# A radix-4 fold of the even half of a d-transform, with the front of the kernel re-ordered around it

## The chip, the cores and the metric

The kernel runs on one core of one Trainium2 chip. The metric is device microseconds for one execution of the program, the median of three runs. Five engines of the core matter here, and the profile's names are used for them: PE (TensorE, matrix products; PEld is its weight loads), DVE (VectorE), ACT (ScalarE), POOL (GpSimd) and SP (SyncE, which issues most DMAs). PE writes its products into PSUM, and DVE or ACT copy them out from there.

## The reference

The kernel computes a gated mix of two branches on the same x (2048 tokens of 1024 features):

```python
g = sigmoid((x * gate_w).sum(-1))
a = irfft2(rfft2(x) * (w_r + 1j * w_i))            # spectral branch
Bu = einsum("bld,pd->blp", x, B_bar)               # state-space branch
h_t = Lam_bar * h_(t-1) + Bu_t                     # for all 2048 tokens
b = 2 * einsum("blp,dp->bld", h, C).real + x * Dskip
out = g * a + (1 - g) * b
```

All inputs and the output are bf16, except that some small parameters come as float32.

## The kernel before

The work of PE, DVE and ACT is emitted inside a guard that keeps each of these three engines to the written order: an instruction that waits holds up everything written after it on its engine. So the order of the Python text is the schedule, and this case is about that order.

**The front, steps 0 to 15.** x is read as 16 blocks of 128 tokens. For each block `turn_x` (L663, letter T) transposes it with eight small PE products into PSUM, and ACT copies it into `xQ`. `fold` (L670, letter f) forms the sum and the difference of the two halves of the feature axis with two DVE instructions of 512 elements a partition (`preT`). `fd` (L342, letter F) is the transform along d: eight products of 512 columns into one PSUM tile `ps_fd`, four for the even class of frequencies (from the sums) and four for the odd class (from the differences), and one copy into `X1` by ACT, or by DVE for blocks 3, 5 and 7. `s1` (L352, letter S) is the first stage of the transform along the tokens: four products into `ps_s1`, one copy into `A1` (by DVE for blocks below 8, by ACT from 8 on), and a DMA of `A1` to DRAM. `front()` (L782) does one step: it walks through the letters of `plan` (L780), where F at step j is the transform of block j+1 and S is the token stage of block j; where the plan has no entry the letters are fFS. Then it issues the loads that `order` (L772) lists for the step, and then it advances `tables` by `pieces`.

`ps_fd`, `ps_s1` and the gate's `zps_g` take turns in one pool of two PSUM buffers, `psA`. A product that opens a buffer waits for the copy that empties the one before it there.

**The tables.** `sincos` (L825) makes sines and cosines in three parts: DVE reduces the angle, ACT does the absolute value and the sine, ACT does the cosine. It is used once for a few small vectors (`s2c`, `c2c`, L844), which feed a chain of about 25 small DVE instructions (L847 to L869), and then in `make_tab` (L210) for four pairs of table rows. Each `make_tab` has five parts: the angle on DVE (L215, L828, L830); absolute value and sine on ACT; cosine and two scalings `t1` on ACT (L226); two scalings `t2` on ACT and two DVE instructions that need `t1` (L232); two DVE instructions that need `t2` (L237).

**The units.** `unit(c, q)` (L301) computes Bu for a chunk c of 256 tokens and one half q of the states: two halves (real, imaginary) of 32 products of 256 columns into `psu`, and an ACT copy into `h`. `halves(ssm, n)` emits the next n halves of a list (L770) in which eight units stand first, and then the `early` tiles, which multiply finished states with C. When a unit is complete, `recur` (L254) puts its recurrence on a list of DVE pieces: two products with the tables, two joins, two scans, the carry, two products, two outputs. Each piece has a cost written down; `vector(us)` (L321) adds us to a budget and emits pieces while the budget is positive. `vector(4.2)` stands in steps 9 to 15, `vector(3.0)` after each of the halves that follow.

**After the front.** `gfnet` goes on with short stages whose names are the letters of L892: four halves of units beside "w"; "a" transposes the saved columns `Acol` into `aps`, from which DVE copies `Bcol` (L423); the first half of `early(0)`; then "z", whose products `zps` (L430) read `Bcol`. In the DVE's order `Bcol` stands behind everything that was written before it: all folds, copies and tables of the front and all pieces that the budget has let out by then.

`keep_A1(j)` (L367) saves columns of four `A1` tiles on DVE before ACT overwrites the first of them at block 12. `gate()` (L708) is emitted at step 10. SP issues its DMAs in the order written: x, the constants G and T2, the transposing loads of B (`load_B`) and of C (`load_C`), and the stores of `A1`.

Of the kernel before, what the change touches and what calls it, by code (L numbers as in the profile page):

```python
# [21 lines left out]
K = 512  # L22
# [15 lines left out]
def _host_consts():  # L38

    d = np.arange(K)[:, None] + 0.5  # L40
    G = np.zeros((2, K, 2, H))
    for cls in range(2):
        k = 2 * np.arange(H)[None, :] + cls
        ang = 2 * np.pi * d * k / D
        G[cls, :, 0] = np.cos(ang)
        G[cls, :, 1] = -np.sin(ang)
    G[0, :, 1, 0] = (-1.0) ** np.arange(K)

    n = np.arange(H)[None, :] + 0.5
    Gi = np.zeros((2, 2, 2, P, H))  # L50
    for cls in range(2):
        for kb in range(2):
            k = 2 * (P * kb + np.arange(P)[:, None]) + cls
            ang = 2 * np.pi * k * n / D
            Gi[cls, kb, 0] = 2.0 * np.cos(ang)
            Gi[cls, kb, 1] = -2.0 * np.sin(ang)
    Gi[0, 0, 0, 0] = 1.0
    Gi[0, 0, 1, 0] = (-1.0) ** np.arange(H)
    Gi /= float(D * S)
    pf = np.arange(P)  # L60
    s1 = (32 * (pf % 64) + 16 * (pf // 64))[:, None, None]
# [36 lines left out]
    return dict(  # L98
        G=b16(G.reshape(2, 4, P, K).transpose(2, 0, 1, 3)),
        Gi=b16(Gi.reshape(8, P, H).transpose(1, 0, 2)),  # L100
        T2=b16(np.concatenate([Ts, Tc, -Ts], axis=2)),
        K3=b16(np.stack([Kc, Ks], axis=1)),
        MT=b16(np.concatenate([-Mim, Mre, Mim], axis=2)),
        KRS=b16(np.concatenate([K2, R2, Sel.reshape(P, 4 * P)], axis=1)),
        JP=b16(np.stack([J, P0], axis=1)),
    )
# [3 lines left out]
def kernel(  # L110
# [78 lines left out]
    xn = [CT[i // 4][:, 2 * (i % 4):2 * (i % 4) + 2, :] for i in range(8)]  # L189
    x_v = x.rearrange("(p j) d -> p j d", j=16)  # L190
    fft = {}
    fft["G"] = pre.tile([P, 2, 4, K], BF16, name="G_sb")
    raw = t3p.tile([P, 6 * D], BF16, name="raw")
    fft["T2"] = raw[:, 0:3 * D].rearrange("p (j m) -> p j m", m=192)

# [141 lines left out]
    def gfnet():  # L337
# [3 lines left out]

        def fd(j):  # L342
            ps = psA.tile([P, 2, K], FP32, name="ps_fd", tag="ps")
            for cls in range(2):
                for d4 in range(4):
                    nc.tensor.matmul(ps[:, cls, :], lhsT=preTs[j][:, 4 * cls + d4, :], rhs=G_sb[:, cls, d4, :],  # L346
                                     start=(d4 == 0), stop=(d4 == 3))
            X1 = gta.tile([P, 2, K], BF16, name="X1")
            (nc.vector.tensor_copy if j in (3,5,7,) else nc.scalar.copy)(out=X1.rearrange("p r (i c) -> p r i c", c=2), in_=ps.rearrange("p c (r i) -> p r i c", r=2))  # L349
            X1s[j] = X1  # L350

        def s1(j):  # L352
# [10 lines left out]
            (nc.vector.tensor_copy if j < 8 else nc.scalar.copy)(out=A1, in_=psa)  # L363
            A1s[j] = A1
            nc.sync.dma_start(out=t1_w[j], in_=A1)

# [291 lines left out]
        yield 3.9  # L658


    preTs = {}

    def turn_x(j):  # L663
        pt = psX.tile([P, 8, P], BF16, name="pt")
# [3 lines left out]
                       in_=pt.rearrange("p d (c q g) -> p d c g q", c=NCH, g=2))  # L668

    def fold(j):  # L670
        preTs[j] = gta.tile([P, 8, P], BF16, name="preT", bufs=3)
        lo, hi = (x_gjq[:, :, d:d + 4, :, j, :].rearrange("p c d g q -> p d g c q") for d in (0, 4))
        to = preTs[j].rearrange("p d (g c q) -> p d g c q", g=2, c=NCH)
        nc.vector.tensor_add(out=to[:, 0:4], in0=lo, in1=hi)  # L674
        nc.vector.tensor_sub(out=to[:, 4:8], in0=lo, in1=hi)  # L675

    A1_4 = gta.tile([P, 4, 2, K], BF16, name="A1", bufs=1)
    idle = A1_4[:, 3, 0]
# [6 lines left out]

    keep_warm(8)
    load_x(0)
    for cls in range(2):
        nc.sync.dma_start(out=fft["G"][:, cls], in_=cG[:, cls])
    load_T2(0, 2)  # L690
    load_x(1)
    load_x(2)
    load_T2(2, 8)
    for i in range(3, 8):
        load_x(i)
    load_T2(8, 16)
    assert step() == "front"
    for j in range(2):
        turn_x(j)
# [66 lines left out]
    def halves(gen, n):  # L766
# [3 lines left out]
    ssm = chain(unit(0, 0), unit(0, 1), unit(1, 0), unit(1, 1), unit(2, 0), unit(2, 1), early(0), early(1), unit(3, 0), early(2), unit(3, 1), early(3), unit(4, 0), early(4), unit(4, 1), early(5), unit(5, 0), early(6), unit(5, 1), early(7), unit(6, 0), unit(6, 1), early(8), early(9))  # L770

    order = {  # L772
        **{j: [(load_B, n)] for j, n in ((2, 1), (3, 1), (4, 1), (5, 2), (6, 2), (7, 2), (8, 2), (9, 2))},
        10: [(load_B, 3), (load_small,)],
        **{j: [(load_C, j - 11)] for j in range(11, 15)},
    }
    at = [0]
    tables = iter(())

    plan = {0: "FSTfTf", 1: "TSFfT", 2: "TFfTS", 3: "TFfTS", 4: "TFfTS", 5: "TFfTS", 6: "TFfTS", 7: "TFfTS"}  # L780

    def front(pieces=0):  # L782
        j = at[0]
# [50 lines left out]
        yield  # L834
        nc.scalar.activation(out=cos_out, in_=kk, func=ACT.Sin, scale=-2.0 * PI_LO, bias=chpi[:shape[0]])

    front()

    ang2 = sp.tile([P, 2, 8], FP32, name="ang2")
    nc.vector.tensor_copy(out=ang2[:, 0], in_=thp)  # L840
    nc.vector.tensor_scalar_mul(out=ang2[:, 1], in0=thp, scalar1=float(TC))
    s2c = sp.tile([P, 2, 8], FP32, name="s2c")
    c2c = sp.tile([P, 2, 8], FP32, name="c2c")
    for _ in sincos(sp, ang2, [P, 2, 8], s2c, c2c, "a2"):  # L844
        front()
# [25 lines left out]
    tables = chain(*(make_tab(jp) for jp in range(4)))  # L871
    while at[0] < 16:
        j = at[0]
        front(0 if j < 4 else 1 if j < 6 else 2 if j < 10 else 3)
        if j >= 8:
            halves(ssm, 1)
        if j >= 9:
            vector(4.2)
        if j == 10:
            gate()  # L880
        if j == 15:
            for _ in tables:
                pass
            tctx.close()
        if j == 7:
            xctx.close()
            pools["u"] = ctx.enter_context(tc.tile_pool(name="psU", bufs=2, space=PSUM, reuse_waits="tile"))
        if j == 3:
            load_Wcols()
# [94 lines left out]
```

## Time and profile before

| | us |
|---|---|
| median of 3 runs | 340.34 (340.12 to 340.48) |
| the profiled execution | 340.26 |
| its span in the trace | 338.5 |
| PE busy | 327.9 (97%) |
| DVE busy | 283.5 (84%) |
| ACT busy | 167.3 (49%) |

The profiled execution is 1.8 us longer than its span; these lie before the first and after the last instruction. A busy PE is not a PE at its peak: the records of its products overlap. So the table says which engines are candidates, and the stretches and the single instructions have to say which one sets the end, and where. Most rows of the trace give a start, a duration, the engine and line, the operation, what it writes and reads, and in square brackets how long the engine sat idle before it and what ended that.

### The profile page before, as it was taken

The numbers are of one execution on the slowest core, as the hardware profiler recorded it, in microseconds if no ns is written. First come the engines' busy times: TensorE is split into PE (matmuls) and PEld (weight loads), VectorE is DVE, ScalarE is ACT, GpSimd is POOL, SyncE is SP. The second block draws the span as 40 slices with busy tenths as digits, with TensorE's granted clock in tenths as the row PEclk, the third lists the DMA queues.
The fourth block names the chain that finished last, engine by engine and source line by source line (L and its number), as shares of the span: only waits on it lengthen the run. The fifth ranks groups of instructions, "written<-read, shape, count | busy, mean of one in ns | idle before, by whom it ended". The sixth has DMA issues, their size and how long they took to land.

```text
span 338.5 us, 6167 instructions
## 1 busy us (share of the span) xinstructions
PE 327.9 (97%) x2446; PEld 212.0 (63%) x2446; DVE 283.5 (84%) x385; ACT 167.3 (49%) x211; POOL 32.7 (10%) x64
## 2 busy tenths in 40 slices
PE   8989899979999999999999999999999999999995
PEld 3445465656985574847566575869945876565552
DVE  2679948999999999999997999199699939999741
ACT  3697598836241245656557452546632243433510
POOL 1382011140000000000000000000000011121410
PEclk9999999999999999999999999999999999999999
DMA  7999999999890346899999955898114004556892
GB/s 268 404 200 144 244 220 213 129 202 263 261 230 11 95 123 145 254 243 282 259 270 242 218 174 151 225 188 217 62 33 122 35 4 71 102 86 124 131 194 102
DMA packets 83581, 58.71 MB, mean 173 GB/s; under 512 B 54328, under 2 KB 74304, under 8 KB 83424
## 3 DMA queue, kind: packets, MB, share of 16 engines
q1 hardware_dynamic: 80304, 55.64, 66.5%
q0 software_dynamic: 3168, 2.66, 8.3%
q8 instruction: 19, 0.31, 0.4%
q14 instruction: 10, 0.08, 0.1%
q10 hardware_dynamic: 80, 0.01, 0.0%
HBM read 30.49 MB, written 17.83 MB: 143 GB/s over the span
## 4 chain that ended last, share of the span: by engine, by line
PE 81%; DVE 13%; ACT 3%; issue 2%; ACTq 0%; DVEq 0%
PE ps_y L580 29%; PE psu L308 28%; PE ps_h L580 4%; PE ps_id L611 4%; PE ps_fd L346 3%; PE ps_is L519 2%; PE ps_is L494 2%; PE ps_s L470 2%; PE ps_is L495 2%; DVE CT L363 2%; PE ps_y L584 2%; DVE h L278 1%; DVE preT L674 1%; PE psw L684 1%; DVE preT L675 1%
## 5 line engine op out<-in xcount | busy, mean ns | idle before, releaser
L308 PE MATMUL psu<-xQ,BT 128*128 128x256 bf16 x1024 | 116.2, 273 | 0.8 <-ACT ye L598 0.5
L308 PEld LDWEIGHTS <-BT 128*128 128x128 bf16 x1024 | 99.0, 98 | 17.4 <-issue 4.5
L580 PE MATMUL ps_y<-CT,h 128*128 128x512 bf16 x448 | 101.3, 379 | 0.0
L580 PEld LDWEIGHTS <-h 128*128 128x128 bf16 x512 | 49.4, 98 | 55.3
L278 DVE TENSOR_TENSOR_SCAN h<-rz,h 128x1024 bf16<-128x1024 f32 x32 | 71.9, 2278 | 0.2
L310 ACT CAST h<-psu 128x1024 bf16<-128x1024 f32 x32 | 32.3, 1010 | 51.0 <-PE psu L308 51.0
L263 DVE TENSOR_TENSOR xQ<-h,tab 128x4096 bf16<-128x4096 bf16 x12 | 27.4, 2287 | 14.2 <-ACT h L310 14.2
L266 DVE TENSOR_TENSOR h<-h,tab 128x4096 bf16<-128x4096 bf16 (+1 forms) x20 | 37.3, 1864 | 0.8
L626 POOL DMA_DIRECT2D BT<-y_scratch x10 | 11.9, 1194 | 238.8 <-DVE BT L620 227.1
L598 ACT ACTIVATE ye<-ps_y,omg 128x512 f32<-128x512 f32 x20 | 12.7, 684 | 43.4 <-PE ps_y L584 35.7
L346 PE MATMUL ps_fd<-G_sb,preT 128*128 128x512 bf16 x128 | 30.4, 379 | 1.6 <-ACT X L349 1.0
L346 PEld LDWEIGHTS <-preT 128*128 128x128 bf16 x128 | 12.0, 97 | 15.5 <-issue 2.8
L472 ACT CAST X<-ps_s 128x1024 bf16<-128x1024 f32 x16 | 16.2, 1014 | 8.7 <-PE ps_s L470 8.7
L667 ACT COPY xQ<-pt 128x1024 bf16<-128x1024 bf16 x16 | 15.6, 1016 | 2.6 <-PE pt L666 2.5
L521 ACT CAST ZT<-ps_is 128x1024 bf16<-128x1024 f32 x16 | 15.5, 1024 | 2.2 <-PE ps_is L519 2.2
L497 ACT CAST C<-ps_is 128x1024 bf16<-128x1024 f32 x16 | 16.1, 1007 | 0.0
L611 PE MATMUL ps_id<-raw,ZT 128*128 128x256 bf16 x128 | 15.9, 273 | 0.0
L349 ACT CAST X<-ps_fd 128x1024 bf16<-128x1024 f32 x13 | 13.2, 1013 | 5.5 <-PE ps_fd L346 5.4
L580 PE MATMUL ps_h<-CT,h 128*128 128x512 bf16 x64 | 14.5, 379 | 0.0
L611 PEld LDWEIGHTS <-ZT 128*128 128x128 bf16 x128 | 12.4, 98 | 2.2
L674 DVE TENSOR_TENSOR preT<-xQ 128x512 bf16<-128x512 bf16 x16 | 7.4, 460 | 5.8 <-ACT xQ L667 5.8
L494 PE MATMUL ps_is<-X,raw 128*128 128x512 bf16 x32 | 12.1, 379 | 0.0
(189 smaller groups left out, 350.0 us busy)
## 6 DMA issues: line engine op xcount, KB each, us to landing
y_scratch<-ye SPq DMA_DIRECT2D x20, 256.0 KB, 2.7
CT<-in_A_x_dram SPq DMA_DIRECT2D x8, 512.0 KB, 5.6
Bb<-turn_scratch SPq DMA_DIRECT2D x16, 256.0 KB, 3.8
turn_scratch<-C SPq DMA_DIRECT2D x16, 256.0 KB, 4.5
raw<-turn_scratch SPq DMA_DIRECT2D x16, 256.0 KB, 4.7
Wb<-in_A_w_r_dram SPq DMA_DIRECT2D x32, 127.8 KB, 4.0
Wb<-in_A_w_i_dram SPq DMA_DIRECT2D x32, 127.8 KB, 3.8
out_dram<-BT SPq DMA_DIRECT2D x14, 256.0 KB, 2.6
```

The costliest lines, as they stand in the source:

```text
L263: nc.vector.tensor_mul(out=tmps["s"], in0=u[:, ::-1], in1=bc(i))
L266: nc.vector.tensor_mul(out=u, in0=u, in1=bc(i))
L278: nc.vector.tensor_tensor_scan(out=seg, data0=rz[:, js.start + j:js.start + j + 4].rearrange("p j t -> p (j t)"), data1=seg, initial=0.0, ...
L308: nc.tensor.matmul(psu[:, j, :], lhsT=BT[4 * q + j][:, ri, d8, :], rhs=xQ[:, c, d8, :], start=(d8 == 0), stop=(d8 == 7))
L310: nc.scalar.copy(out=hs[c][:, ri, 4 * q:4 * q + 4].rearrange("p b (q j) -> p b q j", j=32), in_=psu.rearrange("p b (j q) -> p b q j", j=32))
L346: nc.tensor.matmul(ps[:, cls, :], lhsT=preTs[j][:, 4 * cls + d4, :], rhs=G_sb[:, cls, d4, :], start=(d4 == 0), stop=(d4 == 3))
L472: nc.scalar.copy(out=X2, in_=ps2)
L494: nc.tensor.matmul(psc[:, h, :], lhsT=MT_sb[:, b, 64:192], rhs=UV[0][:, h, :], start=True, stop=False)
L497: nc.scalar.copy(out=C1.rearrange("p h (c i) -> p h c i", c=2), in_=psc.rearrange("p h (i c) -> p h c i", c=2))
L580: nc.tensor.matmul(psy, lhsT=hs[c][:, ri, jb, P * tq:P * (tq + 1)], rhs=CT[ri][:, jb, 512 * dh:512 * (dh + 1)], start=(i == 0), stop=False)
L611: nc.tensor.matmul(pse[:, slot, :], lhsT=ZT_t[:, i, tb, :], rhs=fft["Gi"][:, i, :], start=(kb == 0), stop=(kb == 1))
L667: nc.scalar.copy(out=x_gjq[:, :, :, :, j, :].rearrange("p c d g q -> p d c g q"), in_=pt.rearrange("p d (c q g) -> p d c g q", c=NCH, g=2))
```

## The change

The even half of the transform along d is folded once more. The even class needs the sums of the two halves of the feature axis; its frequencies are themselves split into two classes, which need the sums and the differences of the two halves of those sums. `G` shrinks from 8 blocks of 512 columns to 4 of 512 (odd) and 4 of 256 (even), the odd ones loaded first. `fd` does the odd class first, then four products of 256 columns. `fold` gains two DVE instructions, which run over the pair of blocks at once from block 2 on, and block by block for 0 and 1. With it go other moves: which engine copies what (`X1` of block 7 and `A1` of blocks 6 and 7 go from DVE to ACT), the plan (all turns of x within steps 0 to 4), the loads (eight B loads in steps 1 to 3, T2's second half in step 3), the small sines and cosines (steps 5 and 6 in place of 1 and 2), the tables (steps 7 to 12 in place of 4 to 12), the halves of units (steps 6 to 13 in place of 8 to 15) and the recurrence pieces (from step 8 in place of 9).

```diff
         def fd(j):
             ps = psA.tile([P, 2, K], FP32, name="ps_fd", tag="ps")
-            for cls in range(2):
-                for d4 in range(4):
-                    nc.tensor.matmul(ps[:, cls, :], lhsT=preTs[j][:, 4 * cls + d4, :], rhs=G_sb[:, cls, d4, :],
-                                     start=(d4 == 0), stop=(d4 == 3))
+            Go = G_sb[:, 0:4 * K].rearrange("p (d n) -> p d n", d=4)
+            Ge = G_sb[:, 4 * K:4 * K + 4 * H].rearrange("p (e d n) -> p e d n", e=2, d=2)
+            for d4 in range(4):
+                nc.tensor.matmul(ps[:, 1, :], lhsT=preTs[j][:, 4 + d4, :], rhs=Go[:, d4, :], start=(d4 == 0), stop=(d4 == 3))
+            for e in range(2):
+                for d2 in range(2):
+                    nc.tensor.matmul(ps[:, 0, H * e:H * (e + 1)], lhsT=preTs[j][:, 2 * e + d2, :], rhs=Ge[:, e, d2, :],
+                                     start=(d2 == 0), stop=(d2 == 1))
             X1 = gta.tile([P, 2, K], BF16, name="X1")
-            (nc.vector.tensor_copy if j in (3,5,7,) else nc.scalar.copy)(out=X1.rearrange("p r (i c) -> p r i c", c=2), in_=ps.rearrange("p c (r i) -> p r i c", r=2))
+            (nc.vector.tensor_copy if j in (3, 5) else nc.scalar.copy)(
+                out=X1.rearrange("p r (m e c) -> p r m e c", e=2, c=2),
+                in_=ps.rearrange("p c (e r m) -> p r m e c", e=2, r=2))
...
-            (nc.vector.tensor_copy if j < 8 else nc.scalar.copy)(out=A1, in_=psa)
+            (nc.vector.tensor_copy if j < 6 else nc.scalar.copy)(out=A1, in_=psa)
...
     def fold(j):
-        preTs[j] = gta.tile([P, 8, P], BF16, name="preT", bufs=3)
+        if j % 2 == 0:
+            pairs["t"] = gta.tile([P, 2, 8, P], BF16, name="preT", bufs=2)
+            pairs["s"] = gta.tile([P, 2, 4, P], BF16, name="sums", bufs=1)
+        preTs[j] = pairs["t"][:, j % 2]
...
-        nc.vector.tensor_add(out=to[:, 0:4], in0=lo, in1=hi)
-        nc.vector.tensor_sub(out=to[:, 4:8], in0=lo, in1=hi)
+        nc.vector.tensor_sub(out=apart(preTs[j])[:, 4:8], in0=lo, in1=hi)
+        nc.vector.tensor_add(out=apart(pairs["s"][:, j % 2]), in0=lo, in1=hi)
+        rs = slice(j % 2, j % 2 + 1) if j < 2 else slice(0, 2)
+        if j < 2 or j % 2:
+            s_lo, s_hi = pairs["s"][:, rs, 0:2], pairs["s"][:, rs, 2:4]
+            nc.vector.tensor_add(out=pairs["t"][:, rs, 0:2], in0=s_lo, in1=s_hi)
+            nc.vector.tensor_sub(out=pairs["t"][:, rs, 2:4], in0=s_lo, in1=s_hi)
...
-    load_T2(8, 16)
...
     order = {
-        **{j: [(load_B, n)] for j, n in ((2, 1), (3, 1), (4, 1), (5, 2), (6, 2), (7, 2), (8, 2), (9, 2))},
-        10: [(load_B, 3), (load_small,)],
+        1: [(load_B, 4)],
+        2: [(load_B, 2)],
+        3: [(load_B, 2), (load_T2, 8, 16), (load_Wcols,)],
+        **{j: [(load_B, 2)] for j in range(4, 8)},
+        10: [(load_small,)],
...
-    plan = {0: "FSTfTf", 1: "TSFfT", 2: "TFfTS", 3: "TFfTS", 4: "TFfTS", 5: "TFfTS", 6: "TFfTS", 7: "TFfTS"}
+    plan = {0: "FSTfTf", 1: "TSFfTT", 2: "TFfTST", 3: "TFfTfST", 4: "TFTfST"}
...
-    front()
+    for _ in range(5):
+        front()
...
-    for _ in sincos(sp, ang2, [P, 2, 8], s2c, c2c, "a2"):
-        front()
+    turns = sincos(sp, ang2, [P, 2, 8], s2c, c2c, "a2")
+    next(turns)
+    front()
+    xctx.close()
+    pools["u"] = ctx.enter_context(tc.tile_pool(name="psU", bufs=2, space=PSUM, reuse_waits="tile"))
+    next(turns)
+    front()
+    halves(ssm, 1)
+    next(turns, None)
...
     while at[0] < 16:
         j = at[0]
-        front(0 if j < 4 else 1 if j < 6 else 2 if j < 10 else 3)
+        front({7: 4, 8: 4, 9: 3, 10: 3}.get(j, 2))
+        if j < 14:
+            halves(ssm, 1)
         if j >= 8:
-            halves(ssm, 1)
-        if j >= 9:
             vector(4.2)
         if j == 10:
             gate()
-        if j == 15:
-            for _ in tables:
-                pass
-            tctx.close()
...
+    for _ in tables:
+        pass
+    tctx.close()
```

More of the change, by code (lines that the diff above doesn't have):

```diff
@@ L47, in _host_consts @@
     G[0, :, 1, 0] = (-1.0) ** np.arange(K)
+    Ge = np.stack([G[0, :H, :, e::2] for e in range(2)])
+    Go = np.stack([G[1, :, :, e::2] for e in range(2)], axis=1)
     n = np.arange(H)[None, :] + 0.5
@@ L98, in _host_consts @@
     return dict(
-        G=b16(G.reshape(2, 4, P, K).transpose(2, 0, 1, 3)),
+        G=b16(np.concatenate([Go.reshape(4, P, 4 * K // 4).transpose(1, 0, 2).reshape(P, 4 * K),
+                              Ge.reshape(2, 2, P, H).transpose(2, 0, 1, 3).reshape(P, 4 * H)], axis=1)),
         Gi=b16(Gi.reshape(8, P, H).transpose(1, 0, 2)),
@@ L191 @@
     fft = {}
-    fft["G"] = pre.tile([P, 2, 4, K], BF16, name="G_sb")
+    fft["G"] = pre.tile([P, 4 * K + 4 * H], BF16, name="G_sb")
     raw = t3p.tile([P, 6 * D], BF16, name="raw")
@@ L658, in own_tile @@
         yield 3.9
-    preTs = {}
+    preTs, pairs = {}, {}
     def turn_x(j):
@@ L670, in fold @@
     def fold(j):
-        preTs[j] = gta.tile([P, 8, P], BF16, name="preT", bufs=3)
+        if j % 2 == 0:
+            pairs["t"] = gta.tile([P, 2, 8, P], BF16, name="preT", bufs=2)
+            pairs["s"] = gta.tile([P, 2, 4, P], BF16, name="sums", bufs=1)
+        preTs[j] = pairs["t"][:, j % 2]
         lo, hi = (x_gjq[:, :, d:d + 4, :, j, :].rearrange("p c d g q -> p d g c q") for d in (0, 4))
-        to = preTs[j].rearrange("p d (g c q) -> p d g c q", g=2, c=NCH)
-        nc.vector.tensor_add(out=to[:, 0:4], in0=lo, in1=hi)
-        nc.vector.tensor_sub(out=to[:, 4:8], in0=lo, in1=hi)
+        apart = lambda t: t.rearrange("p d (g c q) -> p d g c q", g=2, c=NCH)
+        nc.vector.tensor_sub(out=apart(preTs[j])[:, 4:8], in0=lo, in1=hi)
[5 more added lines that the diff above has]
+            nc.vector.tensor_sub(out=pairs["t"][:, rs, 2:4], in0=s_lo, in1=s_hi)
     A1_4 = gta.tile([P, 4, 2, K], BF16, name="A1", bufs=1)
@@ L687 @@
     load_x(0)
-    for cls in range(2):
-        nc.sync.dma_start(out=fft["G"][:, cls], in_=cG[:, cls])
+    for part in (slice(0, 4 * K), slice(4 * K, 4 * K + 4 * H)):
+        nc.sync.dma_start(out=fft["G"][:, part], in_=cG[:, part])
     load_T2(0, 2)
@@ L880 @@
             gate()
-        if j == 15:
-            for _ in tables:
-                pass
-            tctx.close()
[L885 to L889, printed above, removed]
+    for _ in tables:
+        pass
+    tctx.close()
     for q in range(4, 8):
```

## The prediction

> **What bounds the kernel now.** I read the busy times by stretch first (columns: PE, PEld, DVE, ACT and POOL busy with instruction counts, granted PE clock, DMA share, GB/s).
>
> ```profile
> 12.35:18.90 6.55, 5.90 (x53) 3.36 (x51) 4.56 (x13) 5.24 (x7) 2.19 (x12) 1.00 1.23 387
> 18.90:41.40 22.50, 20.07 (x157) 10.42 (x155) 22.11 (x56) 16.64 (x24) 8.74 (x15) 1.00 1.12 182
> 41.40:51.67 10.27, 10.27 (x78) 6.90 (x78) 4.76 (x14) 9.98 (x16) 1.83 (x3) 1.00 1.05 205
> 51.67:71.50 19.83, 19.44 (x164) 12.49 (x161) 19.52 (x29) 13.28 (x20) 5.00 (x7) 1.00 1.11 187
> 71.50:104.50 33.00, 31.69 (x275) 24.67 (x275) 31.48 (x47) 15.09 (x16) 0.33 (x4) 1.00 0.93 221
> 104.50:130.00 25.50, 25.50 (x197) 15.76 (x196) 24.38 (x41) 7.32 (x11) 0.00 (x0) 1.00 0.29 85
> 130.00:334.00 204.00, 203.24 (x1462) 133.10 (x1461) 172.41 (x179) 94.05 (x114) 11.95 (x10) 1.00 0.68 161
> ```
>
> From 104.5 on PE has no hole worth naming, so whatever PE starts late there ends late by as much. From 18.9 to 104.5 the DVE is full too, except in 41.4 to 51.67. Next the instructions in order of time, where the two engines meet:
>
> ```profile
> 45.39 0.91 DVE L232 SCALAR_TENSOR_TENSOR tab<-cs_f,cr,t 128x256 bf16<-128x256 f32 x2 [3.26 <-ACT t L226]
> ...
> 71.75 1.01 ACT L363 CAST A<-ps_s 128x1024 bf16<-128x1024 f32 x1 [4.43 <-DVE Acol L371]
> ...
> 72.81 0.61 PE L358 MATMUL ps_s<-X,raw 64*128 64x512 bf16 x4 [1.70 <-ACT A L363]
> ...
> 103.90 0.69 DVE L269 TENSOR_TENSOR h<-h,su 128x1024 bf16<-128x1024 bf16 x1
> 104.51 0.21 DVE L423 COPY Bcol<-aps 32x128 bf16<-32x128 bf16 x1
> 104.75 0.17 DVE L424 TENSOR_SCALAR Bcol<-Bcol 32x64 bf16<-32x64 bf16 x1
> ...
> 105.27 0.56 PE L430 MATMUL zps<-Bcol,K_sb 32*128 32x16 bf16 x16
> ```
>
> At 71.75 ACT waits for the DVE, and PE loses 1.7 us behind it. At 105.27 PE starts zps, which reads Bcol; the DVE finished it at 104.92. The margin is 0.35 us. So the kernel is bound by the DVE's written order up to Bcol and by PE after it. My prediction is when the DVE reaches Bcol in the new order.
>
> **Prices** (start-to-start, from the order of time): a fold half 0.34; an S copy on DVE 1.14, an X copy 1.22; angle, rounding, subtraction of a table 1.7; L232 and L237 0.8 a pair; on ACT a copy 0.95 to 1.0, absolute value 0.54, sine 0.54, cosine 0.69, t1 0.9, t2 0.9. On PE a T takes 0.55, an S 0.55, a half unit 3.55 with its gap. ps_y needs 3.45 for 16 products of 512 columns, psu 3.49 for 32 of 256: 215.6 and 109.1 ns each. An F goes from 1.83 to about 1.35.
>
> **What PE gains.** 16 x 4 products x 106.5 ns = 6.8 us, if PE is what one waits for.
>
> **What the DVE gets.** No pair instruction is in the trace. The nearest row is a fold half with as many elements, 0.34; the ends are 0.31 (half of L269's 0.61 for 1,024 elements) and 0.69 (L830, as many float32 elements). I take 0.34. From 0.34 and 0.61 a half-size one is some 0.07 + 0.135 = 0.21. So 14 x 0.34 + 4 x 0.21 = 5.6 (ends 5.2 and 11.1); at the dear end all waits below stay and Bcol is 5.5 later. Removed: one X and two S copies, 3.5. These go to ACT, which is busy half the time. The five-dimensional X copy is taken at ACT's 1.01 a copy; doubled, it would put about 3 us on the chain below, and I see no gain. Recurrence: the budget is 8 x 4.2 in place of 7 x 4.2 ahead of the same 4 x 3.0. Worked through piece by piece, before reaches Bcol after the first join of chunk 1's second half (L269 above); after lets the second join, the carry and both scans out too: 0.7 + 0.2 + 4.5 = 5.4. So 5.6 - 3.5 + 5.4 = 7.5 us more DVE work stands ahead of Bcol.
>
> **The steps to the first unit.** Queue by queue, each instruction starts at the latest of its engine, its input and its buffer. Steps 0 to 4 now hold 14 turns in place of 10. F(1) starts at 8.7 and F(2) at 13.4, its even products held by the pair sums until 14.85. Then ACT copies X2 and two turns until 17.75, the first of which (16.8) frees the buffer for turn 7, behind which F(3) stands: 17.4 to 18.75. The DVE, done with fold 4 at 16.4, idles until then. From 18.8 it runs: X3 1.2, fold 5 1.36, S2 1.14, folds 6 and 7 2.05, S3 1.15, to 25.7; a wait of 0.7 for F(5), which stands behind five ACT copies from 19.4 on (24.4); from 26.4 X5 1.2, fold 8 0.7, S4 1.14, angle 0.55, fold 9 1.36, S5 1.14, to 32.5. S(6) needs the buffer that S5's copy empties: 32.55. The first unit starts at 33.15; before, at 40.32. That is the visible gain.
>
> **The new wait.** The small cosine is written behind the first half unit's ACT copy. ACT keeps its order: unit until 36.7, copy until 37.8, cosine until 38.1 (before, c2c ended at 21.87). The DVE has only fold 10 (0.7) meanwhile and idles 4.9 us; behind it waits all of the chain of small vectors, tables and recurrence.
>
> **From 38.1 to Bcol, on the DVE.** Small chain 3.2 (21.79 to 25.05 before); folds 11 to 15 5.45; four tables at 3.25 = 13.0; recurrence quarters 12.4 + 12.4 + 12.5, and 8.45 of the fourth = 45.75 (84.86 to 99.92 shows one); Acol 0.35, the Wc chain 1.3, dgD 1.15, gate 0.9. Sum 71.1. Waits: at steps 7 and 8 four table parts are emitted in a row, so L232 waits for ACT's absolute value, sine, cosine and the first t1 with nothing between: 2.35 each (3.26 before, once). At step 10 L237 waits for t2, which stands behind the h, X and A copies: 2.3. At step 11 0.8. Sum 7.8. Bcol: 38.1 + 71.1 + 7.8 = 117.0, against 104.5.
>
> **Can PE hide it?** No, since ACT hands the DVE's lateness on. The DVE comes to table 2's angle at 38.1 + 3.2 + 1.36 (fold 11) + 1.7 + 2.35 + 0.8 (table 0) + 0.7 + 0.1 + 0.8 + 1.7 + 2.35 + 0.8 (step 8) + 5.95 (five recurrence pieces) + 1.36 + 0.8 + 1.7 (step 9) = 63.8. ACT's absolute value waits for that; behind it stand 2.7 of table work, the copy of unit (0,1) and X11. The gate's products need X11's buffer, so PE, done with unit (1,0)'s first half near 62, starts them at 68.4. S(11) needs the gate's buffer, whose copy stands behind table 3's sine: the DVE ends that angle at 63.8 + 2.24 + 0.7 + 0.8 + 2.3 + 0.8 + 1.7 = 72.3, and ACT's 0.54 + 0.54 + 0.95 + 1.1 make it 75.5. From there PE is dense: three halves, three F, three S, then F15, X15, S15; Wrev at 94.3 (86.86 before), two units to 108.8, the first half of early(0) to 112.3. The old stall of 1.70 at S13 is gone, since PE is now the later one there. Then zps waits for Bcol, and comes 12.5 us late. The work after it is the same, and the DVE, 5.4 ahead in its pieces, makes no new stall. **Sum: 340.26 + 12.5 = 352.8 us.** The profiled execution is 0.08 below the median of the runs, which I leave out.
>
> The granted clock is 1.00 in every stretch, and PE's longest wait in the rows is 1.70 us. The Trainium skill, "TensorE: Matmul & The Clock Gate", Part 1: The HAM clock gate, says that an idle window of about 3.4 us halves PE's clock until it has been busy for as long again. By that rule the holes of 6 and 7 us above cost, as an estimate, some 2 us of PE each (half the clock for 3.4 us), inside time that PE waits anyway; by the rows, nothing.
>
> **The other moves.** SP: the four B transposes at step 1 stand behind the store of block 1's A1 (its copy ends at 15.7) and take about 1.4 each, so the stores of blocks 2 and 3 slip by up to a microsecond, which nothing reads before the front is over. The eight B parts for the first unit are issued by 30 and land about 5 later, needed at 33.15 and 38.8; the other eight by 44, needed at 44 and 52. T2's second half is issued near 30 and needed at 44. Less G and the later T2 take 0.64 MB out of the opening: no turn waits for x in my steps, so it gives nothing. POOL's column loads stay at step 3. If B came late instead, the first unit and the cosine would slip by as much.
>
> **Rivals.** (1) The table waits are covered, because ACT runs ahead of my queues: 7.8 less, Bcol 109.2, 345.0 us. For it: ACT is half idle. Against: its order is written, and 45.39 shows the wait already. (2) The DVE does not decide and the 6.8 us arrive: 333.5 us. For it: 41.4 to 51.67 holds 5.5 us of DVE idle that a better order could fill. Against: 7.5 us of work and 4.9 of wait come in; it decides only if the DVE reaches Bcol before 104.5. (3) A gain eaten exactly, the same time: 340.3, Bcol at 104.5 by chance. (4) Pair sums or the X copy at their dear ends, or a slower PE after its holes: 5 to 6 us more, 358.
>
> **How the numbers follow.** The forecast 0.55 (349 to 357: first unit and waits off by 4 in all), rival 1 0.22 (343 to 349), rival 4 0.11, rival 2 0.09, rival 3 0.03. Range 343 to 359, which holds the forecast, rival 1 and half of rival 4. A measurement of this kernel tells about 0.2% from no change; by cases: faster 0.09, same 0.03, slower 0.88.
>
> **What would show it.** Right: first psu near 33; c2c's cosine behind the first h copy, the DVE idle about 5 us ahead of cTC; idle ahead of L232 at two tables; a PE hole of 6 us or more ahead of zps_g; Bcol near 117 with zps right behind; no new holes after. Wrong: zps before 104, or PE waiting there for something other than Bcol; a first unit after 37 would mean that I mis-read the opening.

## The result, and the profile after

After takes **356.2 us** (354.99 to 356.32) beside 340.26 us for before on the same chip (340.12 to 340.48): a ratio of 1.046, 95% interval 1.0436 to 1.0483. The profiled execution of after is 356.13 us with a span of 354.4, 15.9 more than the span of before. The forecast was 352.8 with a range of 343 to 359, and 0.88 on slower.

The first lines of after's page (busy time and share of the span; then the granted clock in 40 slices; then the shares of the chain that ended last):

```profile
PE 327.7 (92%) x2446; PEld 214.1 (60%) x2446; DVE 285.4 (81%) x400; ACT 170.7 (48%) x214; POOL 33.4 (9%) x64
...
PEclk9999999689999699999999999999999999999999
...
PE 69%; DVE 21%; ACT 7%; issue 2%; DVEq 0%; ACTq 0%
```

PE is busy for as long as before (327.9 us there), although its products hold 6.8 us less work at full clock. The clock row explains it: two slices stand at 6, where before has a 9 in every slice. Hence a busy time must be read together with the clock under which it was spent. The chain's share of DVE is 21%; before, the page has 13%.

The busy times of after by stretch (columns as in the prediction):

```profile
18.90:41.40 22.50, 20.64 (x185) 13.78 (x184) 16.25 (x51) 16.95 (x20) 7.89 (x13) 1.00 1.11 213
...
62.00:76.00 14.00, 6.53 (x44) 2.47 (x43) 12.43 (x21) 9.63 (x15) 2.97 (x4) 0.63 1.09 206
...
95.00:117.12 22.12, 17.57 (x146) 13.93 (x145) 21.50 (x36) 5.55 (x6) 0.00 (x0) 0.96 0.67 171
117.12:123.00 5.88, 5.88 (x31) 2.50 (x31) 5.78 (x10) 0.00 (x0) 0.00 (x0) 0.58 0.00 0
130.00:334.00 204.00, 201.57 (x1478) 134.44 (x1477) 174.59 (x179) 97.01 (x119) 9.55 (x8) 1.00 0.63 153
```

The DVE, full in 18.9 to 41.4 before (22.11 of 22.5), has 6.25 us of idle time there now. PE has lost its dense order: 6.53 of 14 us in 62 to 76, and 4.55 us of idle time up to 117.12. Behind 117.12 the granted clock is 0.58 with a PE that is busy all the time. From 130 to 334 PE misses 2.4 us; before, 0.76.

Single instructions of after, in order of time:

```profile
38.77 0.17 DVE L875 TENSOR_TENSOR cTC<-c2c,r_sb 128x8 f32<-128x8 f32 x1 [4.81 <-ACT c2c L854]
...
46.81 0.91 DVE L235 SCALAR_TENSOR_TENSOR tab<-cs_f,cr,t 128x256 bf16<-128x256 f32 x2 [2.23 <-ACT t L229]
...
64.11 0.63 ACT L851 ACTIVATE rot_kk<-ang 128x512 f32<-128x512 f32 x1 [7.01 <-DVE ang L849]
...
68.52 3.60 PE L728 MATMUL zps_g<-xQ,gw 128*32 128x512 bf16 x32 [6.69 <-ACT X L356]
...
116.88 0.19 DVE L432 COPY Bcol<-aps 32x128 bf16<-32x128 bf16 x1
...
117.12 0.57 PE L439 MATMUL zps<-Bcol,K_sb 32*128 32x16 bf16 x16 [4.56 <-DVE Bcol L432]
117.63 5.79 PE L589 MATMUL ps_y<-CT,h 128*128 128x512 bf16 x16
...
197.69 2.29 DVE L266 TENSOR_TENSOR xQ<-h,tab 128x4096 bf16<-128x4096 bf16 x1 [5.49 <-ACT h L313]
...
203.69 0.39 PE L503 MATMUL ps_is<-X,raw 128*128 128x512 bf16 x1 [1.68 <-DVE X L488]
```

The whole 15.9 us can be added up from these rows and those of before. zps starts at 117.12 in place of 105.27: **11.85 us**. The 16 products of ps_y behind it take 5.79 us in place of 3.63 under the lower clock: **2.2 us**. Near 203.7 PE waits 1.68 us (and 2.17 for its weights) for the DVE's X (L488), which had no such wait before: **1.84 us** by the offset between the two kernels, which goes there from 14.03 to 15.87 and stays so to the end.

### The profile page after: what moved, and what is told of

Same layout as the page of the kernel before. It is cut to its first block, busy times and chain, and to the rows that moved or that the text cites. A ratio compares the mean times of both kernels' runs of the same rounds, so it can differ in the third digit from the quotient of the medians.

```text
span 354.4 us, 6189 instructions
## 1 busy us (share of the span) xinstructions
PE 327.7 (92%) x2446; PEld 214.1 (60%) x2446; DVE 285.4 (81%) x400; ACT 170.7 (48%) x214; POOL 33.4 (9%) x64
## 4 chain that ended last, share of the span: by engine, by line
PE 69%; DVE 21%; ACT 7%; issue 2%; DVEq 0%; ACTq 0%
PE ps_y L589 26%; PE psu L311 21%; DVE h L281 4%; PE ps_h L589 4%; PE ps_id L620 3%; DVE h L269 2%; PE ps_is L528 2%; DVE su L266 2%; PE ps_is L503 2%; PE ps_is L504 2%; PE ps_s L479 2%; PE ps_y L593 2%; ACT h L313 1%; ACT xQ L676 1%; PE psw L701 1%
## 5 line engine op out<-in xcount | busy, mean ns | idle before, releaser
L589 PE MATMUL ps_y<-CT,h 128*128 128x512 bf16 x448 | 103.4, 385 | 0.0
L266 DVE TENSOR_TENSOR xQ<-h,tab 128x4096 bf16<-128x4096 bf16 x12 | 27.4, 2287 | 20.4 <-ACT h L313 20.4
L350 PE MATMUL ps_fd<-G_sb,preT 128*128 128x512 bf16 x64 | 17.3, 395 | 2.6 <-DVE ang L218 1.5
L356 ACT CAST X<-ps_fd 128x1024 bf16<-128x1024 f32 x14 | 14.2, 1014 | 3.9 <-PE ps_fd L353 3.7
L620 PE MATMUL ps_id<-raw,ZT 128*128 128x256 bf16 x128 | 15.9, 273 | 0.0
L620 PEld LDWEIGHTS <-ZT 128*128 128x128 bf16 x128 | 12.4, 98 | 2.2
L503 PE MATMUL ps_is<-X,raw 128*128 128x512 bf16 x32 | 12.1, 379 | 1.7 <-DVE X L488 1.7
L487 DVE TENSOR_TENSOR V<-X,Wb 128x1024 bf16<-128x1024 bf16 x16 | 10.9, 679 | 2.9 <-issue 2.9
L367 PE MATMUL ps_s<-X,raw 64*128 64x512 bf16 x64 | 9.7, 380 | 2.7 <-DVE CT L372 1.1
```

Of the source, the lines that this page charges most:

```text
L266: nc.vector.tensor_mul(out=tmps["s"], in0=u[:, ::-1], in1=bc(i))
L350: nc.tensor.matmul(ps[:, 1, :], lhsT=preTs[j][:, 4 + d4, :], rhs=Go[:, d4, :], start=(d4 == 0), stop=(d4 == 3))
L503: nc.tensor.matmul(psc[:, h, :], lhsT=MT_sb[:, b, 64:192], rhs=UV[0][:, h, :], start=True, stop=False)
L589: nc.tensor.matmul(psy, lhsT=hs[c][:, ri, jb, P * tq:P * (tq + 1)], rhs=CT[ri][:, jb, 512 * dh:512 * (dh + 1)], start=(i == 0), stop=False)
L620: nc.tensor.matmul(pse[:, slot, :], lhsT=ZT_t[:, i, tb, :], rhs=fft["Gi"][:, i, :], start=(kb == 0), stop=(kb == 1))
```

## The experiments

The first two take the change apart, the next four its loss; one prices the copies, and the rest try to keep the gain. The runs of one version differ by 1 to 4 us, so its median and its one profiled execution can differ by more than a microsecond; where that matters both are given.

**The transform alone.** The order, loads and copies of the kernel before, with the smaller G, the new fd and the pair instructions of fold. `X1` of block 7 and `A1` of blocks 6 and 7 stay on the DVE. The core of the edit to before:

```diff
-            for cls in range(2):
-                for d4 in range(4):
-                    nc.tensor.matmul(ps[:, cls, :], lhsT=preTs[j][:, 4 * cls + d4, :], rhs=G_sb[:, cls, d4, :],
...
+            for d4 in range(4):
+                nc.tensor.matmul(ps[:, 1, :], lhsT=preTs[j][:, 4 + d4, :], rhs=Go[:, d4, :], start=(d4 == 0), stop=(d4 == 3))
...
+        if j < 2 or j % 2:
+            s_lo, s_hi = pairs["s"][:, rs, 0:2], pairs["s"][:, rs, 2:4]
+            nc.vector.tensor_add(out=pairs["t"][:, rs, 0:2], in0=s_lo, in1=s_hi)
+            nc.vector.tensor_sub(out=pairs["t"][:, rs, 2:4], in0=s_lo, in1=s_hi)
```

> The kernel before with the radix-4 transform alone: same plan, same loads, same copies (X1 of blocks 3, 5, 7 and A1 of blocks below 8 on DVE), same tables and budgets; only G, fd and fold are the new ones. Theory (the DVE's written order up to Bcol sets the end): the pair sums put 14 x 0.34 + 4 x 0.21 = 5.6 us on the DVE ahead of Bcol, nothing on it is removed, so Bcol slides from 104.5 to about 110 and zps waits for it: 340.3 + 5 = about 345. Rival (PE sets the end): 64 products of half width save 6.8 us: 333.5. A time within 1 us of 340.3 would say that the DVE's idle time between 41 and 52 us took the pair sums in.

Measured: 344.35 us, ratio 1.0093 [1.0061, 1.0125]. From its trace:

```profile
74.94 1.04 PE L353 MATMUL ps_fd<-G_sb,preT 128*128 128x256 bf16 x4 [2.78 <-DVE preT L691]
...
77.42 5.49 PE L311 MATMUL psu<-xQ,BT 128*128 128x256 bf16 x32
...
105.98 0.17 DVE L741 CAST gB<-g_bf 128x16 f32<-128x16 bf16 x1 [2.11 <-ACT g_bf L740]
...
110.74 0.56 PE L439 MATMUL zps<-Bcol,K_sb 32*128 32x16 bf16 x16
```

The same place in the trace of before:

```profile
100.51 0.17 DVE L724 CAST gB<-g_bf 128x16 f32<-128x16 bf16 x1 [0.59 <-ACT g_bf L723]
```

The DVE reaches Bcol at 109.97, 5.5 us later than in before, as the theory said, but not by the work of the pair sums (5.6 by the prediction's working). It waits 2.11 us at gB for ACT's g_bf, and ACT comes to that behind its copies of the units, which wait for PE. From gB to Bcol it takes 4.0 us in both kernels, so Bcol follows PE here. And the zps row has no bracket: PE does not wait for Bcol. PE itself is late, because its even products wait for the pair sums (5.2 us in four waits), and because 32 products of 256 columns behind such a wait take 5.49 us in place of 3.67 (the granted clock is 0.50 from 77.4 to 80). So the time is right by luck: the wait that the theory named is not the one that ends last.

**The order alone.** After, with the transform of the kernel before.

```diff
-            for d4 in range(4):
-                nc.tensor.matmul(ps[:, 1, :], lhsT=preTs[j][:, 4 + d4, :], rhs=Go[:, d4, :], ...)
...
+            for cls in range(2):
+                for d4 in range(4):
+                    nc.tensor.matmul(ps[:, cls, :], lhsT=preTs[j][:, 4 * cls + d4, :], rhs=G_sb[:, cls, d4, :], ...)
...
-        if j < 2 or j % 2:
-            s_lo, s_hi = pairs["s"][:, rs, 0:2], pairs["s"][:, rs, 2:4]
-            nc.vector.tensor_add(out=pairs["t"][:, rs, 0:2], in0=s_lo, in1=s_hi)
-            nc.vector.tensor_sub(out=pairs["t"][:, rs, 2:4], in0=s_lo, in1=s_hi)
```

> The changed kernel with the old transform: eight products of 512 columns per block and two fold instructions, but the new plan, loads, copies, tables and budgets. Theory (DVE order): 5.6 us of pair sums leave the DVE, PE gets 6.8 us back; Bcol at about 111.5 in place of 116.9, PE there at about 111, so no hole of a few us and no drop of the clock behind it: about 356.2 - 5.5 - 2.2 = 348.5. Rival (PE sets the end of the changed kernel): 6.8 us slower, 363.

Measured: 355.89 us, ratio 1.0422 [1.0376, 1.0469]. A miss: I had expected the missing 5.6 us of pair sums to be missing from the time. Two rows of its waits (in total, number, longest) and two instructions say where they went:

```profile
DVE X L349 <- PE ps_fd L346: 6.2, 2, 4.0
DVE tab L232 <- ACT t L226: 5.4, 3, 2.2
```

```profile
40.70 0.17 DVE L858 TENSOR_TENSOR cTC<-c2c,r_sb 128x8 f32<-128x8 f32 x1 [5.52 <-ACT c2c L837]
...
117.36 0.56 PE L430 MATMUL zps<-Bcol,K_sb 32*128 32x16 bf16 x16 [3.18 <-DVE Bcol L423]
```

In the opening of the new order the DVE waits for PE and ACT, so work taken from the DVE there becomes a wait (the 6.2 us; in after these waits are 3.0), while every transform that is 0.43 us longer delays PE, the first unit (35.75 in place of 33.81) and with it the small cosine: cTC starts 1.93 us later. Only three pairs of sums, 2.0 us, lie behind the cosine, and a table waits 0.9 us more. Bcol comes at 117.13, where after has 116.88. So **the order by itself makes the loss of after**, and in that order the smaller transform neither helps nor harms. Work on an engine counts only in the stretch where that engine is the late one.

**The cosine earlier.** After, with the small cosine issued right behind the small sine, ahead of the step's front and of the first unit.

```diff
     next(turns)
+    next(turns, None)
     front()
     halves(ssm, 1)
-    next(turns, None)
```

> The changed kernel with one line moved: the cosine of the small angles is written right behind their sine, ahead of step 6, and no longer behind the first half unit's copy. Theory: the DVE's wait of 4.81 us ahead of cTC goes, everything behind it on the DVE moves up, Bcol from 116.9 to about 112.1; PE, which waits on ACT behind the tables, moves up too, so the hole ahead of zps and the slower clock behind it stay: about 356.2 - 4.8 = 351.4. Rival (the table waits on ACT or PE's own work set the pace): the time doesn't move, 356.

Measured: 352.99 us, ratio 1.034 [1.0293, 1.0387]. The wait of 4.81 us is gone, zps comes at 113.21, 3.9 us earlier, and the hole ahead of it stays (4.57): held, at a little less than the wait was long, since a table waits 0.9 us more. The median fell by 3.2 us, the profiled execution by 4.4.

**The pieces later.** After, with the recurrence's budget from step 9, as in before.

```diff
-        if j >= 8:
+        if j >= 9:
             vector(4.2)
```

> The changed kernel with the recurrence budget from step 9, as before, in place of step 8: 4.2 us of budget less ahead of Bcol. Theory: 5.4 us of pieces go from ahead of Bcol to behind it, so Bcol comes at about 111.5; table 2's angle comes 5.9 us earlier, so ACT is not held and the PE hole of 6.7 us ahead of the gate closes; and since the pieces then stand against the later stages as they did before, the PE wait of 1.7 us at L503 near 202 goes: about 356.2 - 5.4 - 1.8 = 349. Rival (that wait near 202 has another cause, such as a load): about 350.8 with the wait still in the trace. Rival (pieces do not matter): 356.

Measured: 348.36 us, ratio 1.0205 [1.015, 1.026]. Two rows of its trace:

```profile
72.25 1.04 PE L367 MATMUL ps_s<-X,raw 64*128 64x512 bf16 x4 [6.00 <-ACT zsb L730]
...
112.82 0.55 PE L439 MATMUL zps<-Bcol,K_sb 32*128 32x16 bf16 x16 [2.02 <-DVE Bcol L432]
```

7.8 us come back by the median, 6.8 in the profiled execution. The 6.8 add up: 4.3 at zps, 0.6 in the products of ps_y behind it (5.17 in place of 5.79), and 1.84 since the wait of L503 near 203 has gone (the DVE waits 14.2 us for h copies in four waits, as in before; in after it is 20.4 in five). One budget of pieces, let out a step early, thus costs twice: it stands ahead of Bcol, and it puts the product of a later chunk in the DVE's queue ahead of work for which PE waits.

**Both.** The two edits above together.

> The changed kernel with both of the moves that paid singly: the cosine right behind the sine, and the recurrence budget from step 9. Theory (two terms of one DVE order that add up): cos_early moved Bcol from 116.88 to 112.97 and pieces_later to 112.56; together Bcol at about 108.6 and, with no wait at L503, a time of about 348.4 - 4 = 344.4, and about 343 if the hole ahead of zps gets too short for the clock to drop. Rival (they close the same gap, since the waits on ACT's table work grow when the DVE comes earlier): 347 to 348.

Measured: 344.79 us, ratio 1.0119 [1.009, 1.0148]; Bcol at 108.97, zps at 109.23 behind a hole of 2.15. The two terms add up: 11.4 of the 15.9 us come from them (10.5 in the profiled execution). The other 4.5 are not traced to a part of the change: the new places of the turns, the loads, the units and the tables were not taken back one by one.

**The hole filled.** After, with 18 products ahead of zps which nobody reads, in the hole where PE waits for Bcol.

```diff
             vector(3.0)
+            if v == "a":
+                psw = psA.tile([P, 2, K], FP32, name="psw", tag="ps")
+                for k in range(18):
+                    nc.tensor.matmul(psw[:, k % 2, :], lhsT=ident, rhs=BT[7][:, 0, 0:4], start=True, stop=True)
```

> The changed kernel with 18 products of 512 columns that nobody reads, written between the first half of early(0) and zps, where PE stands idle for 4.56 us; nothing else is changed. They take 18 x 0.216 = 3.9 us if the clock is full. Theory (the slower clock behind the hole is what made 16 products take 5.79 us in place of 3.63): zps stays at 117.1, the products behind it run at full clock, the time falls by 2.2 us to about 354. Rival (the products there were slow for another reason): the time stays at 356 or grows.

Measured: 354.09 us, ratio 1.0394 [1.0379, 1.0409].

```profile
116.59 0.54 PE L439 MATMUL zps<-Bcol,K_sb 32*128 32x16 bf16 x16 [0.69 <-DVE Bcol L432]
117.06 3.63 PE L589 MATMUL ps_y<-CT,h 128*128 128x512 bf16 x16
```

2.1 us less with 4 us more work on PE: the 16 products take 3.63 us again, and the granted clock behind 117.06 is 1.00. The profiled execution fell by 2.7 us: 2.2 in these products, and 0.5 because Bcol came that much earlier. So the 2.2 are the clock's and not the wait's.

**The copies alone.** The kernel before, with only the moves of the copies: `X1` of block 7 and `A1` of blocks 6 and 7 on ACT.

```diff
-            (nc.vector.tensor_copy if j in (3,5,7,) else nc.scalar.copy)(out=X1...
+            (nc.vector.tensor_copy if j in (3,5,) else nc.scalar.copy)(out=X1...
...
-            (nc.vector.tensor_copy if j < 8 else nc.scalar.copy)(out=A1, in_=psa)
+            (nc.vector.tensor_copy if j < 6 else nc.scalar.copy)(out=A1, in_=psa)
```

> The kernel before with one edit: X1 of block 7 and A1 of blocks 6 and 7 copied by ACT in place of the DVE, as in the change. Theory (DVE order): 3.5 us of work leave the DVE ahead of Bcol; part of it comes back as waits, since PE was at zps only 0.35 us behind Bcol and has 97% of its time full: 339 to 340, PE then the bound at zps. Rival (ACT, 98% busy between 41 and 52 us, takes the copies badly and hands on the delay): 341 to 343.

Measured: 342.45 us, ratio 1.0059 [1.0033, 1.0085]. The rival held:

```profile
39.81 1.89 PE L346 MATMUL ps_fd<-G_sb,preT 128*128 128x512 bf16 x8 [2.49 <-ACT X L349]
```

The DVE has 3.5 us less to do and still reaches Bcol 1.4 us later (105.96), behind a wait of 0.58 us for g_bf and so behind PE. ACT is 48% busy over the span, but in 18.9 to 41.4 the three copies bring it from 16.64 to 19.41 of 22.5 us, and from 30.04 to 40.7 it has no idle time at all. So PE waits 2.49 us for an X copy where it waited 1.03 in before, and all that follows starts later.

**The pair sums on POOL.** The transform alone, with the pair sums from the third pair on GpSimd, the copies on ACT as above, and the loads of W's columns moved off POOL's way (step 11 in place of 3, and their tiles set to zero there).

```diff
-            nc.vector.tensor_add(out=pairs["t"][:, rs, 0:2], in0=s_lo, in1=s_hi)
-            nc.vector.tensor_sub(out=pairs["t"][:, rs, 2:4], in0=s_lo, in1=s_hi)
+            eng = nc.vector if j < 4 else nc.gpsimd
+            eng.tensor_add(out=pairs["t"][:, rs, 0:2], in0=s_lo, in1=s_hi)
+            eng.tensor_sub(out=pairs["t"][:, rs, 2:4], in0=s_lo, in1=s_hi)
```

> The order of the kernel before with the radix-4 transform, the copies of the change (X1 of block 7 and A1 of blocks 6 and 7 on ACT), and the pair sums from the third pair on by POOL in place of the DVE; the two columns of W are loaded at step 11 and their tiles cleared first, so that POOL is free in the front. Theory (DVE order): the DVE loses 3.5 us of copies and gains only 0.83 + 0.68 us of sums, so Bcol comes about 2 us earlier than before's 104.5: 338.3, a little faster than before. Rival (POOL's sums come late, and F waits for them as it waited for the DVE's): a POOL pair instruction over 1 us would hold F by a microsecond per pair: 341 to 345, with waits of ps_fd for POOL in the trace. Rival (PE): 333.5.

Measured: 346.99 us, ratio 1.019 [1.0169, 1.021]; a miss. One of POOL's instructions and PE's product behind it:

```profile
61.80 1.23 POOL L692 TENSOR_TENSOR preT<-sums 128x512 bf16<-128x512 bf16 x1 [3.57 <-DVE sums L687]
...
63.09 0.39 PE L353 MATMUL ps_fd<-G_sb,preT 128*128 128x256 bf16 x2 [1.64 <-POOL preT L692]
```

Such an instruction takes 1.15 to 1.33 us there and 0.42 on the DVE, and PE waits 6.0 us in all for them. The copies on ACT add their own waits. The column loads, which POOL is free to issue before their place in the text, began at 1.97 us, and PE's turn waits 1.8 us for a block of x; that the one caused the other is not shown. The Trainium skill, "GPSIMD Engine Reference", 4.1 Engine selection, puts a two-input instruction on GpSimd at about twice the VectorE's time; here, in bf16, it is 2.7 to 3.2 times.

**The gate later.** Both edits (cosine and pieces), and the gate's products at step 13 in place of 10.

```diff
-        if j == 10:
+        if j == 13:
             gate()
```

> The early cosine and the later pieces together, and the gate's products moved from step 10 to step 13. With the gate at step 10 this version took 344.8 us; PE waits 6.00 us ahead of the token stage of block 11, for the gate's copy, which ACT has queued behind a table that waits for the DVE; ahead of zps it waits another 2.15. Theory (the DVE's order sets the end): the 6.0 us hole closes, but the DVE reaches Bcol as before, near 109, so the hole moves to zps (5 to 8 us there in place of 2.15), with 1 to 2 us of lower clock behind it: 344 to 347. Rival (each PE hole counts for itself): the 6.0 us arrive at the end, 338.8, and zps comes near 103.

Measured: 344.04 us, ratio 1.0096 [1.0062, 1.0129].

```profile
68.13 1.02 PE L350 MATMUL ps_fd<-G_sb,preT 128*128 128x512 bf16 x4 [3.64 <-ACT X L356]
...
107.48 0.57 PE L439 MATMUL zps<-Bcol,K_sb 32*128 32x16 bf16 x16 [3.17 <-DVE Bcol L432]
107.98 4.98 PE L589 MATMUL ps_y<-CT,h 128*128 128x512 bf16 x16
```

The DVE theory held in its time, at the near end of it: the hole of 6.00 ahead of the token stage of block 11 has become one of 3.64 ahead of a transform; but the hole at zps grew from 2.15 to 3.17 (less than the 5 expected), and the median fell by 0.75 us only. Bcol (107.22) came 1.75 us earlier, which is all that can reach the end while zps waits for it; the profiled execution fell by 1.8.

**The order mended.** The same, and a smaller budget behind the four halves beside "w".

```diff
-            vector(3.0)
+            vector(1.0 if v == "w" else 3.0)
```

> The same as the run before (early cosine, pieces from step 9, gate at step 13), and behind each of the four halves beside w only 1.0 us of recurrence pieces in place of 3.0. Theory: 8 us of DVE work go behind Bcol, which then comes near 101 to 102; PE becomes the later one at zps, near 103, with no hole there: 336 to 340. Rival (pieces held back are missed later): the first products with the states, or the stages after the front, wait for recurrences that come 8 us later, and 343 to 347 remain.

Measured: **340.09 us** (339.10 to 340.82, 12 runs) beside 340.6 for before in that session; ratio 0.9973 [0.9954, 0.9993].

```profile
68.77 1.87 PE L350 MATMUL ps_fd<-G_sb,preT 128*128 128x512 bf16 x4 [3.65 <-ACT X L356]
...
101.44 0.21 DVE L432 COPY Bcol<-aps 32x128 bf16<-32x128 bf16 x1
...
105.12 0.56 PE L439 MATMUL zps<-Bcol,K_sb 32*128 32x16 bf16 x16
```

The held-back pieces are not missed: PE has no new wait from 130 to the end (173.24 of 174 us from 160 on, as in before). Bcol is now 3.5 us early, so PE sets the end again, and zps starts 0.15 us before its time in the kernel before. Four small moves have taken back the whole loss; two of them (the gate and the smaller budget) undo no part of the change. At this size the gain over before is at the edge of what can be told.

**The mended order without the smaller transform, and with the late cosine.** The run before with the transform and the fold of the kernel before. Its small cosine stands where the change has it, behind the first unit:

```diff
     next(turns)
-    next(turns, None)
     front()
     halves(ssm, 1)
+    next(turns, None)
```

> The same order as the run before with the transform of the kernel before (eight products of 512 columns, two fold instructions). If PE sets the end in the mended order, the smaller transform is worth what PE gains by it between the opening and zps: 10 to 16 transforms of 0.43 us, so this run is 3 to 6 us slower than the run before, 340 to 345. Rival (the DVE still sets it): the 5.6 us of pair sums are gone and nothing is lost, so it is as fast or up to 4 us faster, 334 to 339.

Measured: 344.25 us, ratio 1.0098 [1.0069, 1.0126].

```profile
40.81 0.17 DVE L858 TENSOR_TENSOR cTC<-c2c,r_sb 128x8 f32<-128x8 f32 x1 [5.52 <-ACT c2c L837]
...
72.24 3.25 PE L346 MATMUL ps_fd<-G_sb,preT 128*128 128x512 bf16 x8 [2.88 <-ACT X L349]
...
110.01 0.56 PE L430 MATMUL zps<-Bcol,K_sb 32*128 32x16 bf16 x16
```

The number falls into the forecast, but it does not price the transform, since two things differ between the runs: this one does not have "the same order". It is 4.2 us slower (4.9 at zps). Of the 4.9, 3.5 are there already at 72.24 (68.77 in the run before), where PE in both runs waits for an X copy behind a table, and ACT there waits 4.57 us for an angle on the DVE. The DVE comes to it late behind cTC, which starts at 40.81 here and at 34.2 in the run before. Only the other 1.4 us, which arise behind that hole, come nearly all from PE's own longer products. So how much of the 6.8 us the smaller transform pays out in the mended order is not shown: no run has the old transform with the early cosine.

With the transform of before and the late cosine, this order is 3.65 us slower than the order of before. The table-bound hole is a cost that also the mended run still has: 3.65 us at 68, and another 1.5 by the lower clock (1.87, 1.06 and 0.84 for products that take 1.03, 0.60 and 0.61 elsewhere in the same trace).

**Fewer pieces in the order of before.** The transform alone, with smaller budgets.

```diff
-            vector(4.2)
+            vector(3.0)
...
-            vector(3.0)
+            vector(2.0 if v == "w" else 3.0)
```

> The kernel before with the smaller transform alone (344.35 us), and fewer recurrence pieces ahead of Bcol: budgets of 3.0 in place of 4.2 at steps 9 to 15 and of 2.0 in place of 3.0 behind the halves beside w, 12.4 us in all. Theory: what made that version slow is the DVE, which reaches the pair sums of blocks 11 and 13 late (PE waits 1.88 and 2.78 us for them, and 2 us more by a lower clock behind); with 1.2 us less ahead of each fold these waits go and PE arrives at zps near 103 to 105 with Bcol in time: 337 to 341. Rival (the DVE's own waits for a table part and for the h copy, 2.05 and 2.18 us, set its time there, not the pieces): 343 to 345.

Measured: 355.94 us, ratio 1.0453 [1.0418, 1.0488]; neither theory's number.

```profile
101.40 0.17 DVE L741 CAST gB<-g_bf 128x16 f32<-128x16 bf16 x1 [5.36 <-ACT g_bf L740]
...
106.16 0.56 PE L439 MATMUL zps<-Bcol,K_sb 32*128 32x16 bf16 x16
...
132.51 3.36 PE L589 MATMUL ps_y<-CT,h 128*128 128x512 bf16 x8 [4.58 <-DVE h L291]
...
331.78 0.61 PE L589 MATMUL ps_h<-CT,h 128*128 128x512 bf16 x1 [5.34 <-DVE h L291]
```

Up to zps the theory mostly holds: the waits for L691 fall from 5.2 to 1.1 us, and zps comes 4.6 us earlier than in the transform alone. But the DVE now has idle time that the withheld pieces could have filled (5.36 us in the first row, 11.1 of 20 us busy from 85 to 105), and the recurrences come too late for their readers: 4.6 us at 132 and 5.3 us at 332, with a lower clock behind both. The mended kernel, in its other order, held back 8 us against before and lost nothing; this one held back 12.4 and lost 14 behind zps.

## Why the prediction was right, point by point

- **What bounds.** Right for after: zps waits for Bcol, and removing DVE work ahead of it (pieces) or a wait (cosine) moves the end. Not quite right for before: there PE does not wait at zps, while the DVE waits 0.59 us at gB behind PE's units, so PE is the later one by a little.
- **Bcol at 117.0**: 116.88. That it fits to 0.12 us is partly luck, as three errors cancel: the DVE starts behind the cosine 0.7 late (38.77 for 38.1), its work takes 1.2 more (72.3 for 71.1), and its waits 2.0 less (5.8 for 7.8).
- **The first unit** (33.15): 33.81. **The cosine** behind the first h copy (38.1, the DVE idle 4.9): 38.74 and 4.81.
- **Table waits** (twice 2.35, then 2.3, then 0.8): twice 2.23, then 1.33, then none. **The pair price** of 0.34: 0.42 a record, 0.34 from start to start.
- **ACT hands the lateness on** (gate at 68.4, the token stage of block 11 at 75.5, Wrev at 94.3): 68.52, 75.54, 94.09.
- **The 12.5 us at zps**: 11.85. The sum let zps slide by as much as Bcol, though in before PE came to zps 0.76 us after Bcol began, and in after only 0.24. The prediction had seen such a margin (0.35) and left it out of its sum.
- **What failed: the clock.** The prediction said that the holes cost PE some 2 us "inside time that PE waits anyway; by the rows, nothing". The hole ahead of zps ends where the waiting ends: the slow products lie behind it, where nothing waits. Filling the hole gave 2.1 us. Its rival 4 had named "a slower PE after its holes"; the forecast had it at nothing.
- **What failed: the stage after.** It said that "the DVE, 5.4 ahead in its pieces, makes no new stall". It is ahead, and for that very reason a piece of the next chunk, which waits for its h copy, stands ahead of the products L487 and L488 that PE needs: 1.84 us. With the pieces from step 9 it is gone.
- **What held but was credited wrongly.** The sum puts 5.6 us of pair sums and -3.5 us of copies ahead of Bcol. As entries of the one total they fit. As causes they do not: without the pair sums the time stays (355.89), and in before's order the copies on ACT cost 2 us instead of saving 3.5. The causes that removal shows are the cosine (3.2 us alone) and the early pieces (7.8); the 4.5 us that are left with both removed have no cause shown.

The two missed terms, 4.0 us, less 0.65 at zps (0.12 for an earlier Bcol, the rest for the margin), are the difference between 352.8 and 356.2.

What stays open: the last table-bound hole in the mended order (ACT waits 4.57 us for an angle on the DVE, PE 3.65 behind it). Without it and its slow products PE would reach zps some 5 us earlier (an estimate from 3.65 and 1.5). Whether Bcol would be there in time is open: at 101.44 it follows PE's own product aps (101.17), so it too would come earlier. This was not tried. The smaller transform's worth in that order is open as well.

## What to carry to other kernels

When engines keep a written order, moving an operation forward moves everything behind it back; price each move by what then stands ahead of the one instruction for which the bounding engine waits, and confirm by taking the move away, not by adding up busy times. A saving on one engine is paid out only in the stretches where that engine is the late one: the smaller transform gave nothing in the order of the change and cost 3.5 us in the order of before. And two versions price a change only if nothing else differs: one line in another place leaves the transform's worth in the mended order open. Let background work out neither too early (it blocks) nor too late (its readers wait, and the idle time it could have filled is lost).

## What the runs showed of the hardware

The granted clock falls behind some holes shorter than I had thought worth pricing, and the length of a hole alone does not say behind which. The 16 products of ps_y behind zps take 3.63 us with no hole or one of 0.69, 5.17 behind 2.02, 5.03 behind 2.15, 4.98 behind 3.17, 5.11 behind 3.18, and 5.27 and 5.79 behind 4.57 and 4.56. So at this place a hole of 2 us cost a further 1.4 to 1.5 us, and one of 4.6 us 1.6 to 2.2. At other places it differs. In before, the products behind 1.70 us run at full speed (0.61 at 72.81). In the run headed "The gate later" they do so even behind 3.64 us (1.02 at 68.13, granted clock 1.00), while in the mended run the same four products behind 3.65 us take 1.87 (granted clock 0.50). The Trainium skill, "TensorE: Matmul & The Clock Gate", Part 1: The HAM clock gate, speaks of an idle window of about 3.4 us that runs freely. That holes of one length end both ways fits a window that runs freely; its length does not fit, since these runs have the loss already behind 2.02 us of idle time, followed by zps's 16 small products. There the measurement decides.
